# A gated long-convolution block followed by an MLP: D loaded in runs, two fetches put off by a phase, and side work moved behind copies

## The chip, the cores and the metric

The kernel runs on one core of a Trainium2 chip. The metric is the device time of one execution in microseconds (us), as a median over runs. The engines of the core are TensorE (PE; its weight loads are listed as PEld), VectorE (DVE), ScalarE (ACT), GpSimd (POOL) and SyncE (SP, which here only issues DMAs). Each engine works through its own instructions in order; DMAs are issued from the queues of SP, ACT and POOL.

## The reference

All arrays are float32; S = 2048 positions, D = 640 channels, F = 1728 hidden units. What matters of the reference:

```python
mod = silu(c) @ w_mod                      # six rows of 640: sa, ca, ga, sb, cb, gb
h  = layernorm(q) * (1 + ca) + sa
ks = causal depthwise convolution of k with 4 taps (shift_k)
kv = ks * v
y  = irfft(rfft(kv, 4096) * rfft(ssm_k, 4096))[:2048]   # per channel, along S
y  = y + kv * ssm_D
x  = q + ga * (h * y)
h  = layernorm(x) * (1 + cb) + sb
x  = x + gb * (relu(h @ w1 + b1) ** 2 @ w2 + b2)
```

## The kernel before

**Stages.** The channels are worked on in five blocks of 128 (b = 0 to 4). For each block, four pieces of 512 positions of k and v are loaded with positions on the partitions, transposed on PE (`kv_k` for k, `kv_v` for v), convolved with the four taps on DVE (`kv_s`), multiplied (`kv_m`) and stored to a scratch tensor in DRAM, `kv_d`. From there (`load_x`), and from ssm_k (`load_h`), both of 1 MB a block, a tile `pt[b]` is loaded with the layout of a two-stage Fourier transform. `skip(b)` adds D to the first tap of ssm_k, which replaces the term kv * ssm_D. `unit_a` is the first stage of the transform (eight units for h, eight for x, in PSUM tiles of the tag X, four buffers), its results are copied by ACT. `front(b, j)` (j = 0 to 7) does the second stage for h and x, and multiplies the spectra: products on DVE, combinations on POOL. `back(b, j)` (j = 0 to 3) does the first stage of the inverse: `qp` in two PSUM tiles of the tag Y (two buffers), copied to the tile q by ACT, and in the last block by DVE for one of the last two. `unit_t` transposes q, eight times a block, ACT copies, and `unit_y` finishes the inverse.

**Gate and side work.** `load_xp(b)` loads a block of columns of q (1 MB), here called gate x; `prep_a` on ACT, `prep_m` on DVE and `prep_p` on POOL turn it into layernorm(q) times modulation, in four pieces; `gate` multiplies it with y. `put_mod` loads the rows of w_mod in five pieces (`part_load`, four buffers of the tag STG), scales them on ACT (`part_scale`), adds them on POOL (`part_add`) and sums over the partitions on PE (`mod_row`, `mod_col`). `w_high` (ACT) and `w_low` (DVE or POOL) split the first MLP weights into a high and a low part ahead of the MLP, which runs in eight chunks of 256 positions and 14 pieces of F, in the second half of the span.

**Order.** The order on every engine is the order in which the program is written; it is kept by `keep_order()`. The main loop runs over the blocks, with ten steps FS(b, j) for `front` and `back` and 18 (11 in the last block) steps GS(b, s) for `unit_t`, `unit_y` and the next block's `unit_a`. A table `tab` says behind which step each side work is issued: `at(GS(1, 1), load_h, 3)` puts block 3's h load behind step 1 of GS in block 1. `put_kv`, `put4`, `put_u` and `put_mod` fill that table; `put_u(b, places)` puts `prep_a` at a place, `prep_m` one step and `prep_p` two steps later. A DMA that has to wait holds back what stands behind it on its queue.

**The start.** Ahead of the main loop block 0 is brought in by hand: SP loads the four pieces of k and v and four pieces of h in turn; POOL loads D in four strided DMAs into the partitions 0, 32, 64 and 96 of `dsm` (four bytes each run), and adds D to each piece of h as it lands; PE takes the transposes of one piece of k and v (`kv_all`) and two units of `unit_a` alternately.

Of the kernel before, what the change touches and what calls it, by code (L numbers as in the profile page):

```python
# [11 lines left out]
F32 = mybir.dt.float32  # L12
# [5 lines left out]
S, D, F = 2048, 640, 1728  # L18
P = 128
NB = D // P  # L20
NL = S // P
NG = 16
DG = P // 4
# [64 lines left out]
def ssm_mlp_kernel(  # L88
# [21 lines left out]
    pe, act, dve, pool, sp = nc.tensor, nc.scalar, nc.vector, nc.gpsimd, nc.sync  # L110
# [11 lines left out]
    sb = ctx.enter_context(tc.tile_pool(name="sb", bufs=1))  # L122
    ps = ctx.enter_context(tc.tile_pool(name="ps", bufs=1, space=bass.MemoryType.PSUM))
# [5 lines left out]
    def copy(eng, o, i):  # L129
        if eng is act:  # L130
            act.activation(o, i, AF.Copy)  # L131
        else:
            eng.tensor_copy(o, i)
# [4 lines left out]
    def add(eng, o, a, b):  # L138
        eng.tensor_add(o, a, b)  # L139
# [29 lines left out]

    ident = sb.tile([P, P], F32, tag="ident", name="ident")  # L170
    make_identity(nc, ident)
    ones = sb.tile([P, P], F32, tag="ones", name="ones")
    dve.memset(ones, 1.0)
    eps_t = sb.tile([P, 1], F32, tag="eps", name="eps_t")
    dve.memset(eps_t, EPS)
    dsm = sb.tile([P, D // 4], F32, tag="dsm", name="dsm")
# [37 lines left out]
    def kv_k(b, h, tag="Y"):  # L214
        acc = KACC[h % 2] if b else K0[:, h]
        t = kt[0] = ps.tile(
            [P, 512], F32, tag=tag, name=f"kt_{b}_{h}", bufs=4 if tag == "X" else 2
        )
        kn = KN[h % (4 if b == 0 else 2)]
        for j in range(4):  # L220
            pe.transpose(t[:, j * P : (j + 1) * P], kn[:, 0, j], ident)  # L221
        act.activation(acc, t, AF.Copy, scale=tap[:, b, 0:1])
        if h < 3:
            copy(act, ktail[:, h % 2, 0:3], t[:, 509:512])

    def kv_s(b, h):
        acc, tk = KACC[h % 2] if b else K0[:, h], kt[0]
        for t in (1, 2, 3):
            parts = [(acc[:, t:], tk[:, : 512 - t])]
            if h:  # L230
                parts.append((acc[:, :t], ktail[:, (h - 1) % 2, 3 - t : 3]))
            for o, x in parts:
                dve.scalar_tensor_tensor(  # L233
                    o, x, tap[:, b, t : t + 1], o, op0=ALU.mult, op1=ALU.add
                )

    def kv_v(b, h, tag="X"):
        t = kt[1] = ps.tile(
            [P, 512], F32, tag=tag, name=f"vt_{b}_{h}", bufs=4 if tag == "X" else 2
        )  # L240
        kn = KN[h % (4 if b == 0 else 2)]
        for j in range(4):
            pe.transpose(t[:, j * P : (j + 1) * P], kn[:, 1, j], ident)  # L243
        n = 4 * b + h + 2
        if 6 <= n < 4 * NB:
            kv_load(n)

    def kv_m(b, h):
        acc = KACC[h % 2] if b else K0[:, h]
        dve.tensor_mul(acc, kt[1], acc)  # L250
        sp.dma_start(kv_d[b * P : (b + 1) * P, h * 512 : (h + 1) * 512], acc)
# [70 lines left out]
    def load_gb():  # L322
        src = gb_d.rearrange("p (g r a f) -> p g r a f", g=16, r=2, a=2)
        for i in range(4):
            sp.dma_start(gb[:, 4 * i : 4 * i + 4], src[:, 4 * i : 4 * i + 4])
        sp.dma_start(gi[0:64, 0], gi0_d.rearrange("f (r n) -> f r n", r=2))
# [12 lines left out]
    AX, QT = {}, {}  # L339
# [5 lines left out]

    def skip(b, i0=0, i1=DG):
        hd = pt[b][:, 1, i0:i1, 0]
        add(dve if b else pool, hd, hd, dsm[:, b * DG + i0 : b * DG + i1])

    def unit_a(b, i, g):  # L350
        t = ps.tile([P, 4, 32, 4], F32, tag="X", name=f"pa_{b}_{i}_{g}", bufs=4)
        for u in range(4):
            w = pt[b][:, i, 4 * g + u, :]
            for r in range(2):
                pe.matmul(t[64 * r : 64 * r + 64, u], w, cw[:, r], start=True, stop=True)  # L355
        o = AX[b][i][:, :, 16 * g : 16 * g + 16].rearrange("p m (u d) -> p m u d", u=4)
        copy(act, o, t.rearrange("p u m d -> p m u d"))

    def spectrum(t, b, i, g, s):
        for r in range(2):  # L360
            for a in range(2):
                pe.matmul(  # L362
                    t[64 * a : 64 * a + 64, s + r],
                    gb[:, g, r, a],
                    AX[b][i][:, 2 * g + a],
                    start=True,
                    stop=True,
                )
# [3 lines left out]
    def early_h(b, j):  # L372
        if j % 4 == 0:
            HS[j // 4] = sb.tile([P, 4, 4, P], F32, tag=f"XP{j // 4}", name=f"hs_{j // 4}")
        if True:
            t = ps.tile([P, 4, P], F32, tag="X", name=f"eh_{b}_{j}", bufs=4)
            spectrum(t, b, 1, 2 * j, 0)
            spectrum(t, b, 1, 2 * j + 1, 2)
            copy(act, HS[j // 4][:, j % 4], t)
# [33 lines left out]
    def back(b, j):  # L413
        if j == 0:
            QT[b] = sb.tile([P, DG, 32, 4], F32, tag="S4", name=f"q_{b}")
        t = [ps.tile([P, 4, P], F32, tag="Y", name=f"qp_{b}_{j}_{a}", bufs=2) for a in range(2)]
        for u in range(4):
            w = ws[b, 2 * j + u // 2]
            for r in range(2):
                for a in range(2):  # L420
                    l = slice(64 * a, 64 * a + 64)
                    pe.matmul(  # L422
                        t[a][:, u],
                        gi[l, 4 * j + u, r],
                        w[r][l, u % 2],
                        start=(r == 0),
                        stop=(r == 1),
                    )
        m = 8 * j
        for a in range(2):  # L430
            copy(
                dve if a and b == NB - 1 and j == 3 else act,
                QT[b][:, :, m + a : m + 8 : 2, :],
                t[a].rearrange("p m (g d) -> p g m d", d=4),
            )


    XPt, UPt = {}, {}
# [345 lines left out]

    act.dma_start(tap, shift_k.rearrange("(b p) t -> p b t", p=P))
    act.dma_start(cw, cw_d.rearrange("p (r m) -> p r m", r=2))
    for a in range(4):
        pool.dma_start(
            dsm[32 * a : 32 * a + 1, :],
            ssm_D.rearrange("(o g a) -> a o g", a=4, o=1)[a],  # L790
        )
    act.activation(rs1[:, 0:1], eps_t, AF.Copy)
    p_tile(0)
# [7 lines left out]
    def kv_all(h):  # L801
        kv_k(0, h)
        kv_s(0, h)
        kv_v(0, h, "T")
        kv_m(0, h)
# [4 lines left out]
    load_gb(0)  # L810
    kv_all(0)
    unit_a(0, 1, 0)
    unit_a(0, 1, 1)
    load_gb(1)
    kv_all(1)
    unit_a(0, 1, 2)
    unit_a(0, 1, 3)
    load_gb(2)
# [12 lines left out]
    for i in range(2):  # L831
        make_gi(2 * i)
        make_gi(2 * i + 1)
        early_h(0, 2 * i)
        early_h(0, 2 * i + 1)
    act.dma_start(ct, c.rearrange("o (b p) -> p (o b)", p=P))
    act.dma_start(ca, ca_d.rearrange("p (r h n) -> p r h n", r=2, h=2))
    for g in range(8):
# [5 lines left out]
    def FS(b, j):  # L844
        return 28 * b + j

    def GS(b, s):
        return 28 * b + 10 + s

    def at(i, fn, *args):  # L850
        tab[i].append((fn, args))

    def each(places, fn, lists):
        for i, a in zip(places, lists):
            at(i, fn, *a)

    def put4(fn, b, places, js=range(4)):
        each(places, fn, [(b, j) for j in js])
# [32 lines left out]
    for b in (3, 4):  # L891
        at(GS(b - 2, 0), p_tile, b)
        put_kv(b, [[GS(b - 2, 4 * h + i) for i in range(4)] for h in range(4)])
        at(GS(b - 2, 1), load_h, b)


    def q_big(tag, l0):
# [19 lines left out]
    each(q_do, stats1, [(l,) for l in range(NL)])  # L917
    at(GS(1, 15), stats1_end)
    at(FS(1, 8), load_xp, 0)
    at(GS(1, 8), load_xp, 1)  # L920


    def put_mod(j, ld, sc, ad, mm, fn, *args):
# [25 lines left out]
        GS(2, 16), mod_col, cbs[:, 0], 0.0)  # L949
    put_mod(4,  # L950
        [FS(3, 0), FS(3, 1), FS(3, 2), FS(3, 3), GS(3, 1)],
        [FS(3, 5), FS(3, 6), FS(3, 7), FS(3, 8), GS(3, 6)],
        [FS(3, 9), GS(3, 0), GS(3, 1), GS(3, 8)],
        GS(3, 11), mod_col, cbs[:, 1], 1.0)

# [1 line left out]
    def put_u(b, places):  # L957
        for j, i in enumerate(places):
            at(i, prep_a, b, j)
            at(i + 1, prep_m, b, j)  # L960
            at(i + 2, prep_p, b, j)
# [12 lines left out]
    put4(finish_add, 1, [FS(3, s) for s in (4, 5, 7)], (1, 2, 3))  # L974
    put4(finish_stats, 1, [GS(3, s) for s in (0, 1, 2)], (1, 2, 3))
    at(GS(3, 3), load_xp, 3)
    put_u(2, [FS(3, 5), FS(3, 7), GS(3, 1), GS(3, 3)])
    put4(gate, 2, [GS(3, s) for s in (3, 4, 5, 6)])
    put4(finish_near, 2, [GS(3, 5), GS(3, 6)])
    put4(finish_add, 2, [GS(3, s) for s in (6, 7, 8)], (1, 2, 3))  # L980
    put4(finish_stats, 2, [GS(3, s) for s in (8, 9, 10)], (1, 2, 3))
    at(GS(3, 11), load_xp, 4)
    put_u(3, [GS(3, s) for s in (9, 11, 13, 15)])
    put4(gate, 3, [FS(4, s) for s in (0, 1, 2, 3)])
    at(FS(4, 1), u_tile, 4)
    put_u(4, [FS(4, s) for s in (2, 4, 6, 8)])
    put4(finish_near, 3, [GS(4, 0), GS(4, 1)])
    put4(finish_add, 3, [FS(4, 9), GS(4, 0), GS(4, 1)], (1, 2, 3))
    put4(finish_stats, 3, [GS(4, s) for s in (2, 3, 4)], (1, 2, 3))
# [36 lines left out]
    def b2_load():  # L1026
# [9 lines left out]
    at(GS(4, 0), w_tile, "S3", 3)  # L1036
    ahead = [
        (GS(3, 7), GS(3, 11), GS(3, 12), dve),
        (GS(3, 8), GS(3, 13), GS(3, 14), dve),
        (GS(3, 9), GS(3, 15), GS(3, 16), dve),  # L1040
        (FS(4, 0), FS(4, 4), FS(4, 9), dve),
        (FS(4, 1), FS(4, 8), GS(4, 1), pool),
        (FS(4, 3), GS(4, 1), GS(4, 3), pool),
# [149 lines left out]
    for i in range(len(seq) + MLAG):  # L1193
        if i >= MLAG:
            n, f = seq[i - MLAG]
# [7 lines left out]
        if i <= last:  # L1203
            n, f = seq[i]
# [42 lines left out]
```

## Time and profile before

| | |
|---|---|
| median of 3 runs | 717.54 us (716.93 to 717.74) |
| the profiled execution | 719.46 us, span 717.7 us |
| granted TensorE clock, mean | 0.995 |
| PE busy | 692.4 us (96%) |
| DVE, ACT, POOL busy | 340.8, 335.9, 294.0 us |
| DMA | 72.62 MB, 100 GB/s of HBM traffic over the span |

The span is the time from the first to the last instruction of the profiled execution. The share of the chain is what the work that ended last waited for, step by step. Where an engine is idle, the profile names what ended the wait; idle time of an engine that others do not wait for costs nothing.

### The profile page before, as it was taken

What the parts mean: (1) busy time and instruction counts of PE and PEld (TensorE: products, weight loads), DVE (VectorE), ACT (ScalarE), POOL (GpSimd) and SP (SyncE); (2) the same over time, 40 slices, a digit from 0 to 9 for tenths busy, and PEclk for the clock granted to TensorE, in tenths of its full rate; (3) what the DMA queues carried; (4) which work ended last, traced back from release to release, by engine and by line L of the source; (5) the groups of instructions that cost most, each with busy time, mean ns of one, the idle gap of its engine ahead of it and who ended that gap; (6) DMA issues with size and microseconds to landing.
All of it is one profiled execution on the core that took longest, in us unless ns stands there. A gap on an engine that the chain in (4) does not pass through costs nothing.

```text
span 717.7 us, 18527 instructions
## 1 busy us (share of the span) xinstructions
PE 692.4 (96%) x7916; PEld 659.9 (92%) x7916; DVE 340.8 (47%) x665; ACT 335.9 (47%) x688; POOL 294.0 (41%) x339
## 2 busy tenths in 40 slices
PE   5899999989999999899999999999999999999996
PEld 4788899879989899789999999999999999999996
DVE  3445675665888589759841331232312312312313
ACT  3545555675893976647633323323323333233221
POOL 2033026146754967934451532422514415325213
PEclk9999999999999999999999999999999999999999
DMA  9797594995465363327410020020020010200101
GB/s 218 203 201 238 151 302 131 251 273 144 117 197 149 109 170 93 118 83 227 137 41 34 1 74 1 2 74 1 2 74 1 37 37 1 74 1 1 38 2 37
DMA packets 88276, 72.62 MB, mean 101 GB/s; under 512 B 19265, under 2 KB 73985, under 8 KB 88193
## 3 DMA queue, kind: packets, MB, share of 16 engines
q1 hardware_dynamic: 86176, 70.83, 35.1%
q8 instruction: 62, 1.02, 0.6%
q10 hardware_dynamic: 1888, 0.60, 0.4%
q14 instruction: 22, 0.17, 0.1%
q0 software_dynamic: 128, 0.00, 0.0%
HBM read 57.01 MB, written 14.42 MB: 100 GB/s over the span
## 4 chain that ended last, share of the span: by engine, by line
PE 88%; DVE 4%; ACT 3%; DMA 2%; POOL 2%; issue 1%; POOLq 0%; DVEq 0%; ACTq 0%
PE acc L747 26%; PE h L677 25%; PE pa L355 8%; PE x L362 5%; PE y L496 5%; PE qp L422 4%; PE h L362 4%; PE t L485 2%; PE h L668 1%; PE kt L221 1%; PE vt L243 1%; PE xtp L642 1%; PE eh L362 1%; DMA dsm<-in_A_ssm_D_dram 1%; DVE KV L233 1%
## 5 line engine op out<-in xcount | busy, mean ns | idle before, releaser
L136 POOL TENSOR_TENSOR mtmp<-mtmp 128x256 f32<-128x256 f32 x112 | 71.9, 642 | 242.3 <-ACT mtmp L709 234.4
L677 PE MATMUL h<-xt,w_S 128*128 128x256 f32 x1290 | 167.0, 281 | 0.2 <-DVE w_S L142 0.2
L677 PEld LDWEIGHTS h<-xt,w_S 128*128 128x128 f32 x1290 | 161.2, 190 | 0.4 <-DVE w_S L142 0.4
L747 PE MATMUL acc<-w_S,hring 128*128 128x320 f32 x960 | 156.8, 311 | 0.2 <-DVE hring L142 0.2
L142 DVE TENSOR_TENSOR hring<-mtmp,hring 128x256 fp32r<-128x256 f32 x112 | 65.1, 581 | 189.5 <-ACT hring L131 189.4
L747 PEld LDWEIGHTS acc<-w_S,hring 128*128 128x128 f32 x960 | 141.8, 188 | 0.7 <-DVE hring L142 0.7
L709 ACT ACTIVATE mtmp<-h,b1t 128x256 f32<-128x256 f32 x104 | 49.3, 474 | 177.6 <-PE h L677 174.6
L355 PE MATMUL pa<-wx,p 128*64 128x128 f32 x1280 | 83.7, 280 | 4.1 <-POOL p L139 3.4
L355 PEld LDWEIGHTS pa<-wx,p 128*64 128x64 f32 x1280 | 70.4, 139 | 11.1 <-issue 4.8
L131 ACT ACTIVATE hring<-mtmp 128x256 fp32r<-128x256 f32 x112 | 46.7, 417 | 45.8 <-POOL mtmp L136 44.2
L131 ACT ACTIVATE a<-pa 128x512 f32<-128x512 f32 x80 | 47.7, 599 | 30.7 <-PE pa L355 30.6
L136 DVE TENSOR_TENSOR wx<-x,wx 128x512 f32<-128x512 f32 x64 | 40.9, 683 | 20.5 <-PE x L362 8.5
L496 PE MATMUL y<-wx,wx 128*64 128x64 f32 x1280 | 45.1, 225 | 3.6 <-ACT wx L131 2.7
L496 PEld LDWEIGHTS y<-wx,wx 128*64 128x64 f32 x1280 | 41.7, 139 | 7.1 <-ACT wx L131 3.8
L142 POOL TENSOR_TENSOR we<-wx 128x256 f32<-128x256 f32 x20 | 15.7, 784 | 74.7 <-DVE wx L136 70.1
L233 DVE SCALAR_TENSOR_TENSOR KV<-kt,tap,KV 128x511 f32<-128x511 f32 (+2 forms) x48 | 35.6, 742 | 21.1 <-ACT ktail L131 19.8
L139 POOL TENSOR_TENSOR wm<-wm,wm 128x640 f32<-128x640 f32 x20 | 31.8, 1589 | 31.4 <-ACT wm L306 31.4
L644 DVE TENSOR_SCALAR we<-xtp,cbs 128x256 f32<-128x256 f32 x35 | 19.0, 544 | 52.0 <-PE xtp L642 52.0
L362 PE MATMUL x<-a,gb 128*64 128x128 f32 x640 | 41.7, 274 | 0.7 <-ACT a L131 0.7
L131 ACT ACTIVATE q<-qp 128x512 f32<-128x512 f32 x39 | 21.2, 595 | 34.8 <-PE qp L422 34.8
L362 PEld LDWEIGHTS x<-a,gb 128*64 128x64 f32 x640 | 35.9, 137 | 1.7 <-ACT a L131 0.9
L362 PE MATMUL h<-a,gb 128*64 128x128 f32 x512 | 34.1, 275 | 0.0
(143 smaller groups left out, 1037.5 us busy)
## 6 DMA issues: line engine op xcount, KB each, us to landing
wm<-in_w_mod_dram SPq DMA_DIRECT2D x25, 320.0 KB, 4.4
KV<-in_A_k_dram SPq DMA_DIRECT2D x20, 256.0 KB, 5.8
KV<-in_A_v_dram SPq DMA_DIRECT2D x20, 256.0 KB, 4.9
xp<-in_A_q_dram SPq DMA_DIRECT2D x5, 1024.0 KB, 7.9
out_dram<-x SPq DMA_DIRECT2D x14, 320.0 KB, 2.2
w1s<-in_B_w_dram SPq DMA_DIRECT2D x13, 320.0 KB, 3.8
w2s<-in_B_w_dram SPq DMA_DIRECT2D x13, 320.0 KB, 3.9
kv_d<-KV SPq DMA_DIRECT2D x16, 256.0 KB, 4.1
```

The costliest lines, as they stand in the source:

```text
L131: act.activation(o, i, AF.Copy)
L136: eng.tensor_mul(o, a, b)
L139: eng.tensor_add(o, a, b)
L142: eng.tensor_sub(o, a, b)
L233: dve.scalar_tensor_tensor(o, x, tap[:, b, t : t + 1], o, op0=ALU.mult, op1=ALU.add)
L355: pe.matmul(t[64 * r : 64 * r + 64, u], w, cw[:, r], start=True, stop=True)
L362: pe.matmul(t[64 * a : 64 * a + 64, s + r], gb[:, g, r, a], AX[b][i][:, 2 * g + a], start=True, stop=True,)
L422: pe.matmul(t[a][:, u], gi[l, 4 * j + u, r], w[r][l, u % 2], start=(r == 0), stop=(r == 1),)
L496: pe.matmul(y[64 * h : 64 * h + 64, 4 * (g % 2) + i], tss[g][:, i, 64 * r : 64 * r + 64], ca[:, r, h], start=(r == 0), stop=(r == 1),)
L677: pe.matmul(hps[n, f][:m], WI[1, f][:, a, b], XT[n][:, x, b], start=(b == 0 and i == 0), stop=(b == NB - 1 and i == 2),)
L709: act.activation(r[:m], h[:m], AF.Relu, bias=b1t[:m, f : f + 1])
L747: pe.matmul(acc[2 * s + i], h[:, a, s * P : (s + 1) * P], w[:, y, i * 320 : (i + 1) * 320], start=(f == 0 and ti == 0), stop=(f == NF - 1 ...
```

## The change

- A second tile `d0` of 128 x 640, zeroed by DVE as its first instruction, takes D from ssm_D in one run per partition: partition 32a gets D from its element a on, so that every fourth element is what block 0 needs; `skip(0)` reads it there. The strided loads into `dsm`, for blocks 1 to 4, are issued on POOL's queue behind the adds of block 0.
- The transposes of k's and v's second piece (`kv_all(1)`) come ahead of the second unit of h's first stage.
- The h load of block 3 moves from GS(1, 1) to FS(2, 0), the gate x load of block 1 from GS(1, 8) to FS(2, 1). On SP's queue both then stand behind block 3's `load_x`, h first.
- In block 3 a gate piece's `prep_a` and a w_mod scaling go behind the last copies of q; later a copy of `w_high` goes behind the copy of a transpose, and two gate pieces and two items of the ahead list go some steps later.
- In the last block the last pair of `qp` goes into PSUM tiles of the tag X, its copies are made in halves, and the gate pieces' products and adds are spread anew, so that DVE's products with h and POOL's combinations of the last spectra come ahead of some of them.

The program has the same matmuls as before; on PE only the one unit of h and the second piece's transposes change places.

```diff
+    d0 = sb.tile([P, D], F32, tag="STG", name="d0", bufs=4)
+    dve.memset(d0, 0.0)
...
     def skip(b, i0=0, i1=DG):
         hd = pt[b][:, 1, i0:i1, 0]
-        add(dve if b else pool, hd, hd, dsm[:, b * DG + i0 : b * DG + i1])
+        if b == 0:
+            add(pool, hd, hd, d0.rearrange("p (g a) -> p g a", a=4)[:, i0:i1, 0])
+        else:
+            add(dve, hd, hd, dsm[:, b * DG + i0 : b * DG + i1])
...
-        t = [ps.tile([P, 4, P], F32, tag="Y", name=f"qp_{b}_{j}_{a}", bufs=2) for a in range(2)]
+        end = b == NB - 1 and j == 3
+        t = [
+            ps.tile(
+                [P, 4, P], F32, tag="X" if end else "Y", name=f"qp_{b}_{j}_{a}", bufs=4 if end else 2
+            )
+            for a in range(2)
+        ]
...
-        for a in range(2):
-            copy(
-                dve if a and b == NB - 1 and j == 3 else act,
-                QT[b][:, :, m + a : m + 8 : 2, :],
-                t[a].rearrange("p m (g d) -> p g m d", d=4),
-            )
+        for g in (slice(0, 16), slice(16, 32)) if end else (slice(0, 32),):
+            for a in range(2):
+                copy(
+                    dve if a and end else act,
+                    QT[b][:, g, m + a : m + 8 : 2, :],
+                    t[a].rearrange("p m (g d) -> p g m d", d=4)[:, g],
+                )
...
     for a in range(4):
         pool.dma_start(
-            dsm[32 * a : 32 * a + 1, :],
-            ssm_D.rearrange("(o g a) -> a o g", a=4, o=1)[a],
+            d0[32 * a : 32 * a + 1, 0 : D - a], ssm_D[a:D].rearrange("(o d) -> o d", o=1)
         )
...
     unit_a(0, 1, 0)
-    unit_a(0, 1, 1)
     load_gb(1)
     kv_all(1)
+    unit_a(0, 1, 1)
     unit_a(0, 1, 2)
...
+    for a in range(4):
+        pool.dma_start(
+            dsm[32 * a : 32 * a + 1, :],
+            ssm_D.rearrange("(o g a) -> a o g", a=4, o=1)[a],
+        )
     act.dma_start(ct, c.rearrange("o (b p) -> p (o b)", p=P))
...
-        at(GS(b - 2, 1), load_h, b)
+        at(FS(2, 0) if b == 3 else GS(2, 1), load_h, b)
...
-    at(GS(1, 8), load_xp, 1)
+    at(FS(2, 1), load_xp, 1)
...
-        [FS(3, 5), FS(3, 6), FS(3, 7), FS(3, 8), GS(3, 6)],
+        [FS(3, 5), FS(3, 6), FS(3, 7), FS(3, 9), GS(3, 6)],
...
-    put_u(2, [FS(3, 5), FS(3, 7), GS(3, 1), GS(3, 3)])
+    put_u(2, [FS(3, 5), FS(3, 9), GS(3, 1), GS(3, 3)])
...
-    put_u(3, [GS(3, s) for s in (9, 11, 13, 15)])
+    put_u(3, [GS(3, s) for s in (9, 11, 13, 17)])
...
-    put_u(4, [FS(4, s) for s in (2, 4, 6, 8)])
+    put4(prep_a, 4, [FS(4, s) for s in (2, 4, 6, 7)])
+    put4(prep_m, 4, [FS(4, s) for s in (3, 6, 7, 8)])
+    put4(prep_p, 4, [FS(4, s) for s in (4, 7, 8, 9)])
...
-        (GS(3, 8), GS(3, 13), GS(3, 14), dve),
-        (GS(3, 9), GS(3, 15), GS(3, 16), dve),
+        (GS(3, 8), GS(3, 16), GS(3, 17), dve),
+        (GS(3, 9), FS(4, 0), FS(4, 1), dve),
```

## The prediction

> **What bounds the kernel now.** I read the page first (busy shares, the chain that ended last), then TensorE's own waits, then around each wait the chain in order of time (rows of start, us, what), the DMA issues of short stretches (size, us to landing), a tile's own view, the table of windows and the timeline.
>
> ```profile
> PE 692.4 (96%) x7916; PEld 659.9 (92%) x7916; DVE 340.8 (47%) x665; ACT 335.9 (47%) x688; POOL 294.0 (41%) x339
> PE 88%; DVE 4%; ACT 3%; DMA 2%; POOL 2%; issue 1%; POOLq 0%; DVEq 0%; ACTq 0%
> ```
>
> TensorE (PE) is busy for 692.4 us of 717.7 and holds 88% of the chain. So the change, which leaves the matmuls as they are, can win only PE's remaining 25.3 us without work, and stretches in which PE runs at a low clock. Nothing is edited in the MLP, the longer half. The edits touch five places; each is costed at PE. The timeline's columns are start, us, engine, line, operation, output and input, count, then [idle before it <- what ended it].
>
> **The start (D in runs; k's second piece ahead of h's second unit).**
>
> ```profile
> 3.23 6.63 DMA dsm<-in_A_ssm_D_dram
> p<-in_A_ssm_k_dram SPq DMA_DIRECT2D x1, 256.0 KB, 6.1
> 1.78 0.50 SPq L798 DMA_DIRECT2D p<-in_A_ssm_k_dram  x1
> 10.38 3.68 PE L355 MATMUL pa<-wx,p 128*64 128x128 f32 x32 [3.40 <-POOL p L139]
> 11.58 0.21 POOL L139 TENSOR_TENSOR p<-p,dsm 128x8 f32<-128x8 f32 x1 [1.25 <-DMA p<-in_A_ssm_k_dram]
> 13.99 0.85 PE L221 MATMUL kt<-ident,KV 128*128 128x128 f32 x4
> 15.67 0.75 DVE L233 SCALAR_TENSOR_TENSOR kacc<-kt,tap,kacc 128x511 f32<-128x511 f32 x1 [6.32 <-ACT ktail L131]
> 17.11 0.66 PE L221 MATMUL kt<-ident,KV 128*128 128x128 f32 x4
> 25.29 0.66 PE L332 MATMUL git<-ident,gb 128*128 128x128 f32 x4 [1.68 <-DVE kacc L250]
> DMA to landing us min/median/max: 4.7/6.4/6.7
> KV<-in_A_k_dram SPq DMA_DIRECT2D x1, 256.0 KB, 3.4
> L139 DVE TENSOR_TENSOR p<-p,dsm x4: 207/207/577, 55.3 to 232.6; 128x32 f32<-128x32 f32 x4
> ```
>
> The fourth load of D lands at 3.23 + 6.63 = 9.86; POOL adds it to h, and PE starts at 10.38, 0.52 after the landing. h's first piece had landed at 1.78 + 6.1 = 7.9. If D comes no later than that, PE starts at 7.9 + 0.52 = 8.4, 2.0 earlier. Each old load is 160 runs of 4 B on one partition; the new ones have the shapes 1x16x40, 1x9x71, 1x11x58 and 1x13x49, so 49 runs in place of 640. No such load is in the trace. Bounds: 6.63 as for the old fourth (landing 9.86), and 3.4, which the first k load took in the same two microseconds. I take 4.7, the fastest old load of D (the 4.7/6.4/6.7 row), as nearest: 3.23 + 4.7 = 7.9, level with h. The zeroing of 128x640 that D now waits for is DVE's first instruction; a few tenths at most.
>
> By the page "DMA: Bandwidth & Descriptors" of the Trainium skill (anatomy of one DMA on the GpSimd path), the number of descriptors costs little beside a nearly constant part. By that, the shorter list would not make D land earlier, which is rival 3; the old loads' 4.7 to 6.7 for the same 640 bytes neither show nor refute it.
>
> Then DVE: from 15.67 it works through k's pieces 2, 3 and 4 back to back until PE, waiting 1.68, gets on at 25.29: 9.6 us, 3.2 each. It begins a piece 1.7 after that piece's transposes do (13.99 to 15.67). With the second piece's transposes after one unit of h instead of two (half of 3.68 = 1.84), they start at 8.4 + 1.84 = 10.2 and DVE at 11.9. Piece 3's transposes come three units of h later, still paced by PE, since h's second piece is added at 11.58: 17.11 becomes 15.1, DVE on it at 16.8, and 16.8 + 2 x 3.2 = 23.2, 2.1 earlier than 25.3. PE's own shift is 2.0. The old-style load of D that remains, for the later blocks, moves to about 17.5 us on POOL's queue, behind the four adds; its first user is DVE at 55.3, but its 640 small runs now run among the stores of k*v: I take off 0.2. **Start: -1.8.** Bounds: -2.5 (all loads of the first 10 us half a microsecond earlier as well) and -0.2 (D at 9.86: piece 3 still starts at 17.11, so DVE wins only 15.67 + 3.2 - 17.11 - 1.7 = 0.1, and the reordering little more).
>
> **Fourth h and second gate x a phase later.** Both are 1 MB loads on SP's queue.
>
> ```profile
> 131.53 6.67 SPq L210 DMA_DIRECT2D KV<-in_A_k_dram  x1
> 139.49 5.50 DMA kv_d<-KV
> 141.79 0.63 PE L221 MATMUL kt<-ident,KV 128*128 128x128 f32 x4 [0.82 <-DMA KV<-in_A_k_dram]
> 145.07 0.69 ACT L222 ACTIVATE KV<-kt,tap 128x512 f32<-128x512 f32 x1 [3.46 <-DMA kv_d<-KV]
> 146.63 1.09 PE L355 MATMUL pa<-wx,p 128*64 128x128 f32 x16
> 148.33 1.15 PE L496 MATMUL y<-wx,wx 128*64 128x64 f32 x32 [0.60 <-DVE KV L233]
> 149.29 0.89 ACT L306 ACTIVATE wm<-wm,sg 128x640 f32<-128x640 f32 x1
> 150.32 1.54 POOL L139 TENSOR_TENSOR wm<-wm,wm 128x640 f32<-128x640 f32 x1 [1.12 <-ACT wm L306]
> 151.89 4.10 DMA wm<-in_w_mod_dram
> 157.43 1.69 PE L496 MATMUL y<-wx,wx 128*64 128x64 f32 x32 [1.99 <-ACT wx L131]
> 159.05 2.40 PE L288 MATMUL mr<-wm,ones 128*128 128x320 f32 x4
> 178.03 1.34 PE L288 MATMUL mr<-wm,ones 128*128 128x320 f32 x4
> 159.00:160.00 1.00, 1.00 (x6) 0.50 1.13 339
> ```
>
> The k load's issue is held for 6.67 us, directly behind h's load; without that, k is there before PE asks for it and the 0.82 goes. The store that took 5.50 has less before it, so the wait of 3.46 on ScalarE (ACT) shrinks to under 1, and DVE's lateness that cost 0.60 goes. The 1.99 is a chain: ACT scales a w_mod piece (149.29), POOL adds it (1.54), which frees a buffer, the next piece takes 4.10, ACT scales that, and only then copies the transposes that y needs. Without its backlog ACT would scale the first piece right after the unit that ends on PE at 147.7 and its copy of about 0.6, and PE is 0.82 earlier: 147.5, 1.8 before 149.29. With a slightly quieter queue y comes 1.9 earlier, at 155.5. PE then asks for it 0.82 + 0.60 earlier, so a gap of 1.99 + 1.42 - 1.9 = 1.5 stays. **-1.9**, bounds -0.8 (k's wait alone) and -3.4 (all three).
>
> After the 1.99 the granted clock (after the busy share in the last row) is 0.50: y takes 1.69 against 1.15, mr 2.40 against 1.34. The price is 0.54 + 1.06 = 1.60. PE also idles 1.68 before 25.29, and its transposes there take the full-clock 0.66; 1.5 is below that. **-1.6**, bounds 0 and -1.6.
>
> The page "TensorE: Matmul & The Clock Gate" of the Trainium skill (Part 1) has the clock halved after an idle window of some 3.4 us. Here 1.99 was enough, and the row decides. By the page alone, rival 2 would have no chance.
>
> Where the loads go: behind the fetch of k*v for block 3 at 163.62, and in front of w_mod pieces that wait for POOL anyway.
>
> ```profile
> 163.62 0.68 SPq L198 DMA_DIRECT2D p<-kv_d  x1
> 174.19 0.21 DVE L139 TENSOR_TENSOR p<-p,dsm 128x32 f32<-128x32 f32 x1
> 177.32 1.17 POOL L142 TENSOR_TENSOR we<-wx 128x256 f32<-128x256 f32 x1
> 181.20 2.06 PE L422 MATMUL qp<-we,gi 64*128 64x128 f32 x32
> DMA to landing us min/median/max: 3.2/6.0/12.7
> ```
>
> h is now read by DVE's skip at 174.19 soon after it lands: a new wait. Behind it on DVE stand x's products, then POOL's combination of them, then PE's qp. Two loads at 6.0 each (the p tile's median) end near 163.6 + 12 = 175.6, a little late. POOL takes the product only at 177.32 and PE the result only at 181.20, so it is free until h lands near 178. The second gate x is read half a phase later still.
>
> **Side work behind the inverse spectra's copies.**
>
> ```profile
> 243.39 1.08 ACT L131 ACTIVATE q<-qp 128x512 f32<-128x512 f32 x2
> 244.53 0.66 PE L485 MATMUL t<-ident,q 128*128 128x128 f32 x4 [1.03 <-ACT q L131]
> 270.47 1.15 PE L496 MATMUL y<-wx,wx 128*64 128x64 f32 x32 [0.73 <-ACT wx L131]
> 291.46 1.71 POOL L139 TENSOR_TENSOR up<-up,s1row 128x512 f32<-128x512 f32 x1
> 292.62 1.78 PE L422 MATMUL qp<-wx,gi 64*128 64x128 f32 x20 [0.77 <-ACT q L131]
> 294.39 0.73 ACT L131 ACTIVATE w_S<-w1s 128x640 fp32r<-128x640 f32 x1
> 294.60 0.94 PE L422 MATMUL qp<-wx,gi 64*128 64x128 f32 x12 [0.19 <-POOL wx L139]
> 296.44 1.50 PE L485 MATMUL t<-ident,q 128*128 128x128 f32 x12 [0.91 <-DVE q L133]
> ```
>
> Before 244.53 ACT does a gate piece and a w_mod scaling ahead of the q copies. With these behind, the copies (1.08) run while PE does its next unit of the same length; a wait of 0.1 stays: **-0.95**. What ACT does later is covered by PE's four buffers of that unit's tag. Before 270.47 a weight copy goes behind the transposes' copy: **-0.65** of the 0.73. In the last block the third pair of qp takes other PSUM buffers, so the 0.77 goes, and POOL's add at 291.46 (1.71) goes behind the combination that qp's second half waits for: qp ends near 294.0 instead of 294.60 + 0.94 = 295.5. But ACT still holds the last gate piece and the weight copy until 294.39 + 0.73 = 295.1, and DVE a product that needs that gate piece, both ahead of the q copies. Half a copy later, t starts at 295.6 to 296.0 against 296.44: **-0.6**. Its bounds are -1.9 (0.77 + 0.19 + 0.91) and +1.0 (the same with rival 2).
>
> **Sum.** 1.8 + 1.9 + 1.6 + 0.95 + 0.65 + 0.6 = 7.5. The profiled execution took 719.46 (span 717.7), 1.92 over the median 717.54. 719.46 - 7.5 = 712.0, so 710.0 as a median.
>
> **Rivals.** (1) The w_mod chain keeps y where it is: its 1.54 and 4.10 stay, and if ACT's scaling moves only with PE, the gap stays near 2 and the clock falls again. Then only 0.8 remains of 3.5: 712.7. For it: the buffers of that chain are untouched; against: ACT's 3.46. Chance 0.15. (2) qp ending early and t starting at 295.6 to 296.0 leave PE idle for 1.6 to 2.0 us in one piece, where there were three short ones; if that halves the clock as 1.99 did, it costs 1.6: 711.6. Chance 0.10. (3) D lands as late as before: 0.2 instead of 1.8, 711.6. Chance 0.06. (4) Slower: the moved h queues behind 1 MB of k*v and DVE stands at its skip. Each microsecond of landing past 178 costs one; to outweigh 7.5 and be 1.4 slower, h must land at 187, some 22 us after its issue, where the longest p load took 12.7: 719.0 or more. Nothing nearer lies on that side; 0.06 with what I overlook. (5) Later loads with a pace of their own take most of the first half's gain back: 716.2 and up, 0.05. That the change does not do what it says is excluded: the built program's order has each move.
>
> **Numbers.** Forecast 0.58, its own range 708.5 (all of 3.4) to 711.1 (0.8 alone). Faster: 0.58 + 0.15 + 0.10 + 0.06 = 0.89; within 0.2% (1.4 us, about what a measurement can tell from no change): 0.05; slower: 0.06. Range: 707.8 (start -2.5 and all of 3.4) to 713.5 (rival 1 and half of rival 3).
>
> **What would show it.** The first h unit on PE near 8.4, released by h's load and not D's; git's wait over near 23.2; no wait for k near 140; a granted clock of 1.00 between 150 and 163; no wait of 1 us for q near 237; t's wait in the last block longer than 0.91 but over earlier. I am wrong if the first unit still waits for D, if y's gap at the end of the second block stays near 2, or if DVE's skip of block 3 stalls past what POOL needs.

## The result, and the profile after

The changed kernel takes 713.0 us (median of 7 runs, 712.45 to 715.37) where the kernel before takes 717.74 (7 runs, 716.93 to 720.35): a ratio of 0.9933, 95% interval 0.9915 to 0.9951. Timed a second time beside other kernels it took 713.33 against 719.11, ratio 0.9929 (0.9904 to 0.9954). It is faster by 4.7 to 5.8 us, inside the predicted range (707.8 to 713.5) and 3.0 above the forecast of 710.0.

The two profiled executions stand further apart than the medians: 719.46 before, 712.45 after, 7.0 us. That is a part of the answer, as will be seen.

The page of the changed kernel: the busy time of TensorE (PE) is the old one (692.4 before), its time without work is what shrank.

```profile
span 710.6 us, 18542 instructions
PE 691.7 (97%) x7916; PEld 659.7 (93%) x7916; DVE 339.1 (48%) x667; ACT 336.2 (47%) x689; POOL 297.3 (42%) x343
```

The timeline of the changed kernel, in the same columns as before (start, us, engine, line, operation, output and input, count, [idle before it <- what ended it]), at the places that the prediction named:

```profile
8.47 0.22 POOL L139 TENSOR_TENSOR p<-p,d 128x8 f32<-128x8 f32 x1 [4.45 <-DMA d<-in_A_ssm_D_dram]
8.74 1.97 PE L360 MATMUL pa<-wx,p 128*64 128x128 f32 x16 [1.81 <-POOL p L139]
DMA to landing us min/median/max: 4.7/4.9/5.1
23.06 0.66 PE L334 MATMUL git<-ident,gb 128*128 128x128 f32 x4 [1.44 <-DVE kacc L252]
152.46 1.15 PE L508 MATMUL y<-wx,wx 128*64 128x64 f32 x32 [0.83 <-ACT wx L131]
153.54 1.34 PE L290 MATMUL mr<-wm,ones 128*128 128x320 f32 x4
171.11 0.22 DVE L139 TENSOR_TENSOR p<-p,dsm 128x32 f32<-128x32 f32 x1 [3.40 <-issue]
194.78 1.15 PE L508 MATMUL y<-wx,wx 128*64 128x64 f32 x32 [0.50 <-DVE KV L235]
237.29 0.66 PE L497 MATMUL t<-ident,q 128*128 128x128 f32 x4
261.35 2.42 PE L508 MATMUL y<-wx,wx 128*64 128x64 f32 x64
272.36 0.94 PE L433 MATMUL qp<-we,gi 64*128 64x128 f32 x12 [0.29 <-POOL we L139]
286.18 0.94 PE L433 MATMUL qp<-wx,gi 64*128 64x128 f32 x12 [0.19 <-POOL wx L139]
288.41 2.64 PE L497 MATMUL t<-ident,q 128*128 128x128 f32 x12 [1.29 <-ACT q L131]
290.97 1.60 PE L508 MATMUL y<-wx,wx 128*64 128x64 f32 x32
```

Reading it in order of time, by how much earlier the same row starts than before. The first h unit: 10.38 to 8.74, 1.64, still released by D's landing (8.22). git's wait is over 2.23 earlier, the last y of the second block 4.97 earlier (157.43 to 152.46). Its gap is 0.83 where it was 1.99; no wait for k near 140 is left. mr takes 1.34 again in place of 2.40. So 6.34 is won at the y of 194.78, in spite of its wait, which was 0.28 before. Without the waits of 1.03 and 0.73 the fourth block's end brings 7.85 at 263.6; around a new wait of 0.29 some is lost, and the rows that follow start 7.30 earlier (282.50 for 289.80). In the last block the three waits of 0.77, 0.19 and 0.91 are down to 0.19 and 1.29: t starts 8.03 earlier. Then t takes 2.64 for what took 1.50, and y 1.60 for 1.15: the clock fell. By windows (the value after the five engines' busy times is the granted clock):

```profile
154.00:158.00 4.00, 4.00 (x62) 3.48 (x62) 2.39 (x6) 2.12 (x5) 1.54 (x1) 1.00 0.89 289
158.00:163.00 5.00, 5.00 (x92) 4.83 (x90) 3.63 (x7) 2.21 (x4) 4.40 (x8) 1.00 0.71 190
288.00:291.00 3.00, 2.59 (x14) 2.29 (x14) 3.00 (x4) 1.67 (x5) 3.00 (x3) 0.60 0.00 0
```

The clock is 1.00 between 154 and 163, where before it had been 0.50 from 158 to 161; it is 0.60 from 288 to 291, at rows that had run at 1.00. Both executions pay one such drop ahead of the MLP, each in another place. The MLP's first rows start 6.45 earlier.

An execution without a kept timeline shows only its mean clock. Of the 14 profiled executions behind this document, the five in which TensorE runs at half clock for a while ahead of the MLP have a mean of 0.995 to 0.997, the nine others 0.999 or 1.000. So a mean of 0.997 or less is read below as the sign of such a drop; where it fell is known only for the profiled ones.

### The profile page after: what moved, and what is told of

It is laid out like the page before. It is cut to its first block, busy times and chain, and to the rows that moved or that the text cites. A ratio compares the mean times of both kernels' runs of the same rounds, so it can differ in the third digit from the quotient of the medians.

```text
span 710.6 us, 18542 instructions
## 1 busy us (share of the span) xinstructions
PE 691.7 (97%) x7916; PEld 659.7 (93%) x7916; DVE 339.1 (48%) x667; ACT 336.2 (47%) x689; POOL 297.3 (42%) x343
## 4 chain that ended last, share of the span: by engine, by line
PE 90%; DVE 4%; ACT 2%; DMA 2%; issue 1%; POOL 1%; POOLq 0%; DVEq 0%; SPq 0%; ACTq 0%
PE acc L759 26%; PE h L689 25%; PE pa L360 9%; PE y L508 5%; PE qp L433 5%; PE x L367 5%; PE h L367 4%; PE t L497 3%; PE kt L223 1%; PE h L680 1%; PE vt L245 1%; PE xtp L654 1%; DVE KV L235 1%; PE gr L1035 1%; DMA d<-in_A_ssm_D_dram 1%
## 5 line engine op out<-in xcount | busy, mean ns | idle before, releaser
L136 POOL TENSOR_TENSOR mtmp<-mtmp 128x256 f32<-128x256 f32 x112 | 71.8, 641 | 242.2 <-ACT mtmp L721 232.5
L136 DVE TENSOR_TENSOR wx<-x,wx 128x512 f32<-128x512 f32 x64 | 40.9, 681 | 19.3 <-PE x L367 10.1
L131 ACT ACTIVATE q<-qp 128x512 f32<-128x512 f32 (+1 forms) x40 | 21.3, 584 | 36.1 <-PE qp L433 36.1
```

The source lines that it names most:

```text
L136: eng.tensor_mul(o, a, b)
```

## The experiments

All medians in us, each beside the kernel before in its own group of runs.

| kernel | median | before | ratio (95% interval) |
|---|---|---|---|
| the change | 713.0 | 717.74 | 0.9933 (0.9915 to 0.9951) |
| the change, again | 713.33 | 719.11 | 0.9929 (0.9904 to 0.9954) |
| start only | 715.84 | 718.18 | 0.9971 (0.9953 to 0.9988) |
| k's order only | 718.09 | 717.6 | 1.0008 (0.9993 to 1.0023) |
| fetch only | 716.55 | 718.18 | 0.9977 (0.9963 to 0.9991) |
| fourth h only | 715.32 | 717.6 | 0.9971 (0.9959 to 0.9984) |
| fourth block's side work only | 717.16 | 718.18 | 0.9986 (0.9972 to 0.9999) |
| last block only | 719.38 | 718.18 | 1.0023 (1.0008 to 1.0038) |
| change, gate piece ahead | 712.84 | 719.11 | 0.9917 (0.9895 to 0.994) |
| change, k first | 711.48 | 719.11 | 0.9898 (0.9875 to 0.9921) |
| change, both of these | 711.98 | 719.11 | 0.9905 (0.9882 to 0.9929) |
| change, h in the middle | 711.3 | 717.6 | 0.9914 (0.9899 to 0.9929) |
| change, h in the middle, k first | 710.58 | 717.6 | 0.9898 (0.9882 to 0.9915) |

### The four parts of the change, each alone

**The start** (the kernel before, with these edits of the change):

```diff
+    d0 = sb.tile([P, D], F32, tag="STG", name="d0", bufs=4)
+    dve.memset(d0, 0.0)
...
     unit_a(0, 1, 0)
-    unit_a(0, 1, 1)
     load_gb(1)
     kv_all(1)
+    unit_a(0, 1, 1)
```

> The kernel before with only the start's edits (D in runs, k's second piece ahead of h's second unit). Theory, that the gain is the two waits' shift: the first h unit moves from 10.38 to about 8.7, the wait for git from 25.29 to about 23.1, all later rows shift by 2.1, and the idle before the y at 157.4 stays 1.99 with its halved clock; the median is 2.1 below the kernel before. Rival, that loads and stores with a pace of their own take it back within the first half: under 0.7 below.

Measured: 2.1 less by the ratio (0.9 to 3.4). The timeline of this kernel:

```profile
8.65 1.98 PE L360 MATMUL pa<-wx,p 128*64 128x128 f32 x16 [1.92 <-POOL p L139]
23.37 0.66 PE L334 MATMUL git<-ident,gb 128*128 128x128 f32 x4 [1.44 <-DVE kacc L252]
155.28 1.15 PE L501 MATMUL y<-wx,wx 128*64 128x64 f32 x32 [1.70 <-ACT wx L131]
156.36 1.34 PE L290 MATMUL mr<-wm,ones 128*128 128x320 f32 x4
```

The first unit is where it was expected, and the gain reaches the end. The gap before y is still there, but after 1.70 the clock held (mr in 1.34): the expectation of a halved clock was wrong here.

**k's order alone** (of the start, only the move of `unit_a(0, 1, 1)`; D loaded as before):

> The kernel before with only k's second piece ahead of h's second unit, D loaded as before. Theory, that D sets the first unit and the order sets VectorE's chain: the first unit at 9.6 to 10.4 as before, git's wait over 0.5 to 0.9 earlier than it was beside the same first unit; 0.2 to 0.9 below the kernel before, and D's shape makes up the rest of the start's 2.1. Rival, that the order brings the whole: git's wait over near 23.3 and 1.8 to 2.1 below.

Nothing is won: between 0.5 less and 1.6 more. The timeline:

```profile
10.12 1.97 PE L355 MATMUL pa<-wx,p 128*64 128x128 f32 x16 [3.16 <-POOL p L139]
24.26 0.66 PE L332 MATMUL git<-ident,gb 128*128 128x128 f32 x4 [1.44 <-DVE kacc L250]
155.15 1.15 PE L496 MATMUL y<-wx,wx 128*64 128x64 f32 x32 [2.34 <-ACT wx L131]
156.23 2.31 PE L288 MATMUL mr<-wm,ones 128*128 128x320 f32 x4
```

D still sets the first unit, at 10.12. git is 1.0 earlier than before, but at the end of the second block the gap is 2.34, and after it the clock halves (mr in 2.31). This execution is shorter than the profiled one of before (717.18 against 719.46), the median is not; 8 of its 12 executions have a mean clock of 0.997 or less, against 10 of 22 of the kernel before. Whether the order's gain goes into that drop was not taken apart. What is settled is that the order alone does not bring the start's 2.1, so D's shape has a part in it: the first theory holds there, and its 0.2 to 0.9 for the order is not seen, though up to 0.5 is not excluded. D's shape without the order was not run.

**The fetch** (the kernel before, with both loads moved), and **the fourth h alone** (the first of the two lines):

```diff
-        at(GS(b - 2, 1), load_h, b)
+        at(FS(2, 0) if b == 3 else GS(2, 1), load_h, b)
...
-    at(GS(1, 8), load_xp, 1)
+    at(FS(2, 1), load_xp, 1)
```

> The kernel before with only the fourth h and the second gate x fetched later. Theory, that the queue is freed: no wait for k at 141.8, none at 148.3, a gap under 1 us before the last y of that block, no halved clock there; 2.8 less from the waits and 1.6 from the clock, 4.4 in a profile that fell at 0.50 before. If the clock falls there only in some executions, the median wins less than the profile: 2.8 to 4.4. Rival, that the moved h makes VectorE late in block 3: 1 us or less is won and a wait of PE appears near 178.

> The kernel before with only the fourth h fetched later, the second gate x staying where it was. Theory, that the held k load stood behind h alone: no wait for k at 141.8, the gap before the last y of that block about 1.0, VectorE stands 3 to 5 for h near 171 and TensorE's waits near 197 to 201 grow from 0.3 to about 1.4; 1 to 2 below the kernel before, as the two loads moved together. Rival, that the gate x fills the queue as well: the gap before that y stays above 1.6, and under 0.7 is won.

Measured: 1.7 less (0.6 to 2.7) for both loads, 2.1 (1.1 to 2.9) for h alone. The timeline of both, then that of h alone:

```profile
153.70 1.15 PE L496 MATMUL y<-wx,wx 128*64 128x64 f32 x32 [0.94 <-ACT wx L131]
173.00 0.21 DVE L139 TENSOR_TENSOR p<-p,dsm 128x32 f32<-128x32 f32 x1 [4.06 <-issue]
193.94 0.66 PE L243 MATMUL vt<-ident,KV 128*128 128x128 f32 x4 [0.47 <-DVE KV L250]
197.03 1.15 PE L496 MATMUL y<-wx,wx 128*64 128x64 f32 x32 [0.97 <-DVE KV L233]
```

```profile
155.36 1.15 PE L496 MATMUL y<-wx,wx 128*64 128x64 f32 x32 [1.66 <-ACT wx L131]
174.21 0.21 DVE L139 TENSOR_TENSOR p<-p,dsm 128x32 f32<-128x32 f32 x1 [3.60 <-DMA p<-in_A_ssm_k_dram]
197.86 1.15 PE L496 MATMUL y<-wx,wx 128*64 128x64 f32 x32 [0.68 <-DVE KV L233]
```

With both loads moved the waits for k and for VectorE in the second block are gone, the last gap is 0.94, and the clock holds. That part went as the theory said, and in the other executions too: one of 12 has a mean clock of 0.997 or less, against 18 of 35 of the kernel before beside it. The 2.8 to 4.4 did not come. VectorE (DVE) stood 4.06 at h's skip (the profile names only "issue" there; with h alone it names h's load, 3.60), and TensorE waited 0.47 and 0.97 for VectorE 20 to 25 us later, where 0.28 was. The rival had named the right engine, 16 to 19 us too early. With h alone the gap before y is 1.66: the gate x does fill the queue too, as that rival said, but the wait given back is smaller as well (0.68), and the clock held in 11 of 12 executions (12 of 22 for the kernel before beside it), so h alone is worth no less.

**The side work of the fourth block** (the kernel before, with the moved w_mod scaling, two gate pieces and two weight copies):

```diff
-        [FS(3, 5), FS(3, 6), FS(3, 7), FS(3, 8), GS(3, 6)],
+        [FS(3, 5), FS(3, 6), FS(3, 7), FS(3, 9), GS(3, 6)],
...
-    put_u(3, [GS(3, s) for s in (9, 11, 13, 15)])
+    put_u(3, [GS(3, s) for s in (9, 11, 13, 17)])
...
-        (GS(3, 8), GS(3, 13), GS(3, 14), dve),
-        (GS(3, 9), GS(3, 15), GS(3, 16), dve),
+        (GS(3, 8), GS(3, 16), GS(3, 17), dve),
+        (GS(3, 9), FS(4, 0), FS(4, 1), dve),
...
```

> The kernel before with only the side work of the fourth block moved (one w_mod scaling, two gate pieces, two weight copies behind the copies of the inverse spectra). Theory: the waits at 244.5 (1.03) and 270.5 (0.73) go, a new one of 0.3 for GpSimd's combination comes near 280; 1.2 to 1.5 below the kernel before. Rival, that the moved pieces return as a wait in the last block: 0 to 0.5.

Measured: 1.0 less (0.1 to 2.0). Both waits are gone from the timeline, and the new one is there:

```profile
156.40 1.15 PE L496 MATMUL y<-wx,wx 128*64 128x64 f32 x32 [1.84 <-ACT wx L131]
157.48 2.30 PE L288 MATMUL mr<-wm,ones 128*128 128x320 f32 x4
275.72 1.35 DVE L142 TENSOR_TENSOR w_S<-w1s,w_S 128x640 fp32r<-128x640 f32 x1
276.35 1.31 POOL L139 TENSOR_TENSOR we<-wx 128x256 f32<-128x256 f32 x1
277.71 0.94 PE L422 MATMUL qp<-we,gi 64*128 64x128 f32 x12 [0.29 <-POOL we L139]
```

The first two rows belong to the question of the clock: y comes after 1.84 and still takes 1.15, and only what follows, mr (2.30) among it, runs at half speed. The last three belong to the new wait: GpSimd's (POOL) combination for qp takes 1.31 here and 0.72 in the kernel before, beside the weight split on VectorE that the edit moved into this stretch (1.35).

**The last block** (the kernel before, with `back`'s other buffers and halved copies, and the gate pieces of block 4 moved):

```diff
...
-    put_u(4, [FS(4, s) for s in (2, 4, 6, 8)])
+    put4(prep_a, 4, [FS(4, s) for s in (2, 4, 6, 7)])
+    put4(prep_m, 4, [FS(4, s) for s in (3, 6, 7, 8)])
+    put4(prep_p, 4, [FS(4, s) for s in (4, 7, 8, 9)])
```

> The kernel before with only the last block's edits (other PSUM buffers and halved copies for the last pair, GpSimd's additions moved). Theory, that the waits fall but gather in one gap after which the clock halves: qp ends about 1 us earlier, t starts 0.5 to 1.0 earlier after a gap of 1.3 to 2.0, t x12 takes about 2.6 in place of 1.50; the median lies between 0.5 below and 1.0 above the kernel before. Rival, that the clock does not halve for such a gap: 0.6 to 1.7 below.

This part alone makes the kernel slower: by 1.7 us (0.6 to 2.7), where the theory's upper end was 1.0. Its timeline:

```profile
290.46 0.94 PE L428 MATMUL qp<-wx,gi 64*128 64x128 f32 x12 [0.19 <-POOL wx L139]
290.37 2.48 POOL L139 TENSOR_TENSOR up<-up,s1row 128x512 f32<-128x512 f32 x2
291.59 1.81 DVE L136 TENSOR_TENSOR up<-up,g1row 128x512 f32<-128x512 f32 x1 [2.46 <-ACT up L461]
293.88 1.61 PE L492 MATMUL t<-ident,q 128*128 128x128 f32 x12 [2.48 <-DVE q L133]
295.42 1.98 PE L503 MATMUL y<-wx,wx 128*64 128x64 f32 x32
```

qp ends early, but VectorE has the product of the last gate piece ahead of its half of the q copies; that product stood 2.46 for ScalarE (ACT) and then took 1.81 beside GpSimd's additions. The gap is 2.48, the clock falls during the rows that follow (y in 1.98). The rows ahead of these waits start 2.94 earlier than in the kernel before, t only 2.56: 0.4 is lost there, and t 0.5 to 1.0 earlier, as the theory had it, did not come. The rest fits the clock: 11 of the 12 executions have a mean of 0.997 or less, against 18 of 35 of the kernel before beside it. In the whole change the same gap is 1.29 to 1.30: the product took 0.69 there. Which of the other parts makes it shorter, and how, was not taken apart.

### Variants of the change

**The last gate piece ahead** of the third pair's copies, where ScalarE had idled 1.93:

```diff
+            if last and j == 7:
+                prep_a(b, 3)
             if j % 2 and j >= 3:
                 back(b, j // 2 - 1)
...
-    put4(prep_a, 4, [FS(4, s) for s in (2, 4, 6, 7)])
+    put4(prep_a, 4, [FS(4, s) for s in (2, 4, 6)], (0, 1, 2))
```

> The changed kernel again, to be timed beside the kernels of this group. Theory: a median near 713.0 against 717.7 to 718.2 of the kernel before, 4.7 to 5.2 less, with a mean clock of 0.996 in the executions in which the transposes of the last block run at half clock and near 1.00 in the others; the former are 1 to 1.7 longer. Rival: length and clock of an execution have nothing to do with each other, and the spread comes from the loads of the start.

> The changed kernel with the last gate piece of the last block (four ScalarE instructions, 1.64 us) moved ahead of the third pair's copies, where ScalarE idled 1.93, so that the fourth pair's copies follow its matmuls at once. Theory, that the late copies make the gap after which the clock halves: the wait before t x12 falls from 1.29 to 0.5 or less, t x12 takes 1.50 in place of 2.64, y 1.15 in place of 1.60; 0.8 less where the clock held anyway, 2.4 less where it halved: 0.8 to 2.4 below the changed kernel. Rival, that GpSimd's and VectorE's work sets t's start and the moved piece delays them: within 0.5 of the changed kernel.

The change again gave the median expected; the two executions with a mean clock of 0.996 took 713.99 and 714.36, the four with 0.999 took 713.03 to 713.58. Its profiled execution has the same gap as the first one, and no drop of the clock. The variant's timeline stands below it:

```profile
172.94 0.21 DVE L139 TENSOR_TENSOR p<-p,dsm 128x32 f32<-128x32 f32 x1 [4.64 <-issue]
193.77 0.66 PE L245 MATMUL vt<-ident,KV 128*128 128x128 f32 x4 [0.47 <-DVE KV L252]
196.85 1.15 PE L508 MATMUL y<-wx,wx 128*64 128x64 f32 x32 [0.97 <-DVE KV L235]
290.47 1.50 PE L497 MATMUL t<-ident,q 128*128 128x128 f32 x12 [1.30 <-ACT q L131]
```

```profile
287.92 0.94 PE L433 MATMUL qp<-wx,gi 64*128 64x128 f32 x12 [0.64 <-POOL wx L139]
289.50 1.50 PE L497 MATMUL t<-ident,q 128*128 128x128 f32 x12 [0.64 <-DVE q L133]
```

t's wait is halved, but GpSimd's combination for qp comes later: 0.64 in place of 0.19. Two gaps of 0.64 stand where 0.19 and 1.30 stood: 0.2 won. None of the six executions shows a mean clock under 0.998, but neither does any of the six of the next variant, k first, whose gap before t is 1.31; so that the shorter gap kept the clock up is not shown. The median is 0.5 below the changed kernel, within the noise (the two intervals largely overlap). In the wait the rival was nearer.

**k's second piece ahead of h's first unit:**

```diff
     kv_all(0)
-    unit_a(0, 1, 0)
     load_gb(1)
     kv_all(1)
+    unit_a(0, 1, 0)
     unit_a(0, 1, 1)
```

> The changed kernel with k's second piece ahead of h's first unit as well. Theory, that VectorE's chain over k's pieces sets the end of the start: its second piece starts at about 10.5 in place of 12.6, its last product ends near 21 in place of 23.0, git's wait of 1.44 and the wait for k*v (0.80) go: 1.5 to 2.5 below the changed kernel. Rival, that the loads have a pace of their own (the second v piece lands after 8.7, or the third and fourth pieces come late): within 0.5 of the changed kernel, with a new wait for v or k on TensorE.

> The changed kernel with both of these moves. Theory, that they add up: 2.3 to 4.9 below the changed kernel, 708 to 711. Rival, that the second move's gain is taken back before the last block: as the first move alone.

1.85 below the changed kernel in the same group (710.03 to 712.08 against 713.03 to 714.36), with the gap that was to go still there. The timeline of k first:

```profile
7.67 1.12 PE L223 MATMUL kt<-ident,KV 128*128 128x128 f32 x4 [0.95 <-DMA KV<-in_A_k_dram]
9.61 0.75 DVE L235 SCALAR_TENSOR_TENSOR kacc<-kt,tap,kacc 128x511 f32<-128x511 f32 x1 [0.38 <-ACT ktail L131]
15.74 0.75 DVE L235 SCALAR_TENSOR_TENSOR kacc<-kt,tap,kacc 128x511 f32<-128x511 f32 x1 [2.89 <-ACT ktail L131]
22.20 0.66 PE L334 MATMUL git<-ident,gb 128*128 128x128 f32 x4 [1.44 <-DVE kacc L252]
```

VectorE starts on the second piece at 9.61 (12.58 in the change), but then stands 2.89 for the third, whose transposes come after four units of h: of the 3.0 won, 0.9 reaches git (1.5 against the change's second profile, with git at 23.69). TensorE's gain is, by these rows, the work that it does from 7.67 on, while D is under way. Both moves together gave 711.98, no better than this one alone.

**The fourth h in the middle**, behind block 3's last k*v store, and the same with k first:

```diff
-        at(FS(2, 0) if b == 3 else GS(2, 1), load_h, b)
+        at(GS(1, 15) if b == 3 else GS(2, 1), load_h, b)
```

> The changed kernel with the fourth h fetched three inverse-spectrum slots earlier than in the change (behind the last store of block 3's k*v, ahead of the fetch of k*v), still behind all of that block's k and v loads. Theory, that the fetch's gain is taken back by VectorE, which stands 3.4 to 4.6 for h at its skip and is then late with the next k chain: the stand goes, TensorE's waits of 0.47 and 0.97 near 194 and 197 fall to 0.3 or less in sum, and k's and y's waits of the block before stay away; 1.0 to 1.3 below the changed kernel. Rival, that those two waits are made by the gate pieces' own chain (ScalarE, VectorE, GpSimd) whatever h does: the stand goes and the waits stay; within 0.5 of the changed kernel.

> The same, with k's second piece ahead of h's first unit too. Theory, that the two are independent: 1.8 (as k's second piece brought by itself) and 1.0 to 1.3 together, 710.2 to 710.6 where the changed kernel takes 713.3. Rival, that one of them gives the other's gain back: 711.5.

Timeline of the first:

```profile
152.47 1.15 PE L508 MATMUL y<-wx,wx 128*64 128x64 f32 x32 [1.28 <-ACT wx L131]
168.33 0.21 DVE L139 TENSOR_TENSOR p<-p,dsm 128x32 f32<-128x32 f32 x1
194.19 1.10 PE L508 MATMUL y<-wx,wx 128*64 128x64 f32 x32
```

VectorE no longer stands for h, and with it both of TensorE's waits near 194 and 197 are gone, as the theory said. The median is 2.0 below the changed kernel's second timing; by the ratios to the kernel before, which differed between the two groups, it is 1.1, as expected, with intervals that overlap. With k first the median is 710.58, the lowest of all, 7.0 below the kernel before; but its ratio of 0.9898 is that of k first alone, so it is not shown that the two gains add. Its timeline speaks against the theory in part:

```profile
168.28 0.21 DVE L139 TENSOR_TENSOR p<-p,dsm 128x32 f32<-128x32 f32 x1
171.50 1.34 PE L290 MATMUL mr<-wm,ones 128*128 128x320 f32 x4 [0.69 <-POOL wm L139]
195.11 1.15 PE L508 MATMUL y<-wx,wx 128*64 128x64 f32 x32 [0.80 <-DVE KV L235]
```

VectorE does not stand for h here either, and yet the same y waits 0.80 for it again (0.97 in the second profile of the change); against the kernel with h alone in the middle, VectorE stands 0.5 longer for a gate piece of ScalarE (2.63 for 2.08), and a product and a sum of gate pieces take longer on it (1.65 for 0.97, 1.77 for 0.42). So the stand for h is not needed for that wait: by these rows the gate pieces' own chain, which the rival named, can make it too.

## Why the prediction was right in sign and 3 us too low

**Start: -1.8, measured -2.1.** D's loads took 4.7 to 5.1, as taken. They were issued 0.35 later (1.85 in place of 1.50) behind the zeroing, so D landed at 8.2 and not at 7.9. h had landed at 6.9, so "released by h's load and not D's" was wrong, and the first unit started at 8.74 instead of 8.4. It took 1.97 and not 1.84, and VectorE began k's second piece at 12.58, 0.7 later than said; but the third piece, which sets the end, came as said (transposes at 15.13, VectorE at 16.61), and git at 23.06 was predicted at 23.2. Rival 3 falls: in all seven kernels that load D in runs, GpSimd adds it at 8.3 to 8.7, in the six that load it in 4-byte pieces at 9.4 to 10.1, with medians to landing of 4.7 to 5.1 and 5.4 to 6.4. The page "DMA: Bandwidth & Descriptors" of the Trainium skill (anatomy of one DMA on the GpSimd path) has the list's length cost little beside a nearly constant part; here the list of 49 runs landed about 1 us sooner than that of 640, and the measurement decides. Why is open: before and after, the profile counts 128 packets on GpSimd's DMA queue for the four loads, so it does not itself show a shorter list.

**Fetch: -1.9, measured -2.1, and 1.2 of it given back.** From the start of block 0's x units to the last y of the second block it is 124.8 to 126.0 us in the five kernels that have both loads at the old places, 123.1 to 123.6 in those that have both moved: 2.1 apart. Rival 1 falls. The step that failed is the last: h landed in time, at 171 to 173, but not harmlessly. "Free until h lands near 178" followed one reader (the skip, its products, GpSimd, qp) and not what else waits in VectorE's queue. Behind the products stand the gate pieces, and behind those k's and v's pieces of the next block; VectorE, which stood 3.4 to 5.0 for h, reached these late too. The waits go with h's place: 0.28 to 0.30 in the five profiles with h early, 0.5 to 1.9 in the seven with h late. But of the two with h in the middle, where VectorE does not stand, one has none and the other 0.80, so how much of the late kernels' waits is the stand's is not settled. Across the six profiles with both loads late, TensorE's waits between 170 and 200 are 0.2 to 1.6 above the old 0.28, in the middle about 1.15. The profiled execution of the change paid least (0.50), which made the profile look better than the median: it is the shortest of the change's 13 executions although it holds a clock drop. It begins as rival 4 does, with VectorE standing at its skip, but reaches TensorE by another path, and costs about a sixth of the 7.5 that rival 4 had to outweigh.

**Clock: -1.6, right in the profile, about half of that in the median.** The gap of 1.99 cost 1.6 in the profiled execution. But means of 0.994 to 1.00 stand side by side for the same kernel: of 68 further executions of the kernel before, 35 had a mean clock of 0.997 or less, and their median is 719.11 against 717.45 for the other 33. That fits the price of 1.6; what was wrong is that the sum put the drop into every execution. The conversion then counted it double: the profiled 719.46 lay 1.92 above the median partly because it held that drop, and the sum took the drop off whole and kept the 1.92.

**Fourth block: -0.95 and -0.65, measured -1.0 (0.1 to 2.0).** Both waits went as costed. What was missed is that a weight split, moved into the next block's first combinations, stands beside GpSimd's work for qp: a wait of 0.29, around which 7.85 falls to 7.30. That GpSimd is slower because of the split is read from the rows, not tested by itself.

**Last block: -0.6, measured +1.7 alone.** In the change itself t started about as early as said (8.03 against 7.30 just before: 0.73), after one long gap in place of three, and then rival 2 came true in some executions: of the 13 of the change, five had a mean clock of 0.996, with a median of 714.36 against 713.03 for the other eight. The bound of +1.0 was named, and the chance of 0.10 for the drop was low for this kernel. The share is not a constant of the gap: in the three variants with the same gap (1.30, 1.30 and 1.31) only one of 16 executions had a mean of 0.997 or less.

**The sum.** 2.1 for the start, 2.1 - 1.15 for the fetch, 0.8 for the clock (half of 1.6), 1.0 for the fourth block, and 0.73 less 5/13 of 1.6 in the last: 5.0, against 4.7 and 5.8 measured. So of the 7.5 predicted, the fetch lacks 1.0, the clock 0.8, the fourth block 0.6 and the last block 0.5, and the start has 0.3 more. This is an account from rows of several profiles, not a measurement of each term in one kernel; alone, the four parts gave 2.1, 1.7, 1.0 and -1.7, in sum 3.1. That is less than the whole, but the four intervals are each some 2 us wide; what of it is noise and what is the last block's part, which is worse without the others, is not separated. That the result lies inside the range is in part luck: the upper end of 713.5 was built from rivals 1 and 3, and neither came true.

## What to carry to other kernels

A clock drop read from one profiled execution is an event with a frequency: weigh the term by how many of the executions show it, and don't convert to the median by an offset that holds the same event. When a load is moved so that an engine stands for it, follow that engine's whole queue to its next deadline, even 20 us on, not only the reader of the load. Three short waits gathered into one can be worth less than their sum, when the one is long enough for the clock to fall.

## What the runs showed of the hardware

The length of TensorE's gap did not decide alone whether its clock halved. At the end of the second block gaps of 1.84, 1.99 and 2.34 were followed by the half clock, and gaps of 1.66, 1.70 and 1.89 were not; in the last block those of 2.48 and 1.29 were, and three of 1.30 and one of 1.31 were not. The gaps of 1.44 to 1.68 before git, in all 14 profiles, were not (its transposes took 0.65 to 0.66). Each drop cost 1.5 to 1.6. In windows of 1 us, the clock's shortfall adds up to 1.7 us in each of the five drops, which is 3.4 us at half clock, however long the gap before it was. The page "TensorE: Matmul & The Clock Gate" of the Trainium skill (Part 1) describes a free-running window, which would make it a matter of phase; the scatter agrees with that, while its 3.4 us of idle was not needed in any of these cases.

VectorE's product of the last gate piece (128x512, L136) took 0.69 in the changed kernel and 1.81 in the one with the last block's edits alone; GpSimd added pieces of the same shape beside both, so what makes the difference is not shown.
